# First token's scores and softmax on VectorE, the fourth batch's loads behind w2, and the first w2 piece in halves

## The chip, the cores and the metric

The kernel runs on one core of one Trainium2 chip. The metric is the device time of one execution in microseconds (us), taken as the median of three runs. An execution is also recorded by the hardware profiler; its rows are shown below. The engines are named as in the profile: PE is TensorE (matrix products; PEld its weight loads), DVE is VectorE, ACT is ScalarE, POOL is GpSimd, SP is SyncE, which issues most of the transfers (DMA).

## The reference, cut to what matters

Three layers run one after the other over 4 batches of 576 tokens. An attention through 32 memory slots per head comes first, then a mixture of 8 experts of which each token uses one, then a gated convolutional feed-forward layer.

```python
a = softmax(phi, axis=2)                     # 4 batches, 8 heads, 576 tokens, 32 slots
k_m = einsum('bhsm,bhsd->bhmd', a, k)        # head size 64
v_m = einsum('bhsm,bhsd->bhmd', a, v)
x = softmax(q @ k_m.T / 8) @ v_m             # heads side by side: 4 x 576 x 512
for b in range(4):                           # experts: 512 -> 1024 -> 512
    for s in range(576):
        fresh = argmax(x[b, s] @ w_gate)
        e = fresh if s == 0 or local_gate[b, s] < 0.5 else prev
        out[b, s] = p[e] * (relu(x[b, s] @ w1[e]) @ w2[e]); prev = e
h = relu(out @ w_in)                         # 512 -> 1024
y = (h * sigmoid(conv3(h))) @ w_out          # 3-tap convolution over the tokens, 1024 -> 512
```

The first token of a batch settles which expert is used from then on, until a token's local gate is below 0.5.

## The kernel before

**Work.** The kernel works out the first token's expert of each batch early, loads that expert's weights and runs the whole batch through it (tokens of other experts are treated at the end, by code that the change does not touch). A batch b has two units u = 2b and 2b + 1 of four heads each. For a unit, `phi` is loaded (128 x 576), its softmax is taken (`pmax`, `pexp`, `prec`), PE transposes it (`pback`, PSUM tile `pa`) and multiplies it with keys and values (`mem`, 40 matmuls of which the profile prints one or two groups, PSUM tile `pk`). ACT copies `pk` to `pm`, scaled by the softmax's sums; PE transposes that for both units (`back`, `pkt`), and the copy `vt` holds keys and values by slot. `gatew` multiplies the values with the gate's weights (`pw`, copied to `vwg`).

**First token.** `frow` multiplies the first token's queries with `vt` on PE (`pfa`); DVE scales and masks the 8 x 128 result (`fw`) and takes its maximum (`fmx`). `fexp` takes ACT's exponential and DVE's reciprocal (`fsm`, `fsl`). `fcol` turns the weights into a column with a second product (`pfb`, copied to `fcol`). `flog` multiplies it with `vwg` (`pfc`), takes the maximum (`flm`) and its index `e0i`. SP reads `e0i` to address the expert's weights.

**All tokens.** `scores` (PSUM tile `sc`), then a softmax over slots on DVE and ACT (`st`, `mx`, `sd`, `smx`, `at`), whose result is split into a high and a low part (`att`), because every large product is computed in three products of such parts. `vw` multiplies the expert's first weights with `vt` (`pv`, split into `vh` and `vl`). A hidden product (`h`) is six matmuls into `ph`; ACT's ReLU gives its high part, DVE its low part. A second product (`y`) is 24 matmuls into `py`, which ACT copies out as `ys`. The second weights come in four pieces `wb{batch}_{0..3}` of 512 KB; a load lands in a raw tile (`wb_2r` is the raw tile of piece 2), of which there are six, and `split` makes the parts: ACT the high one, DVE the low one.

**Order.** PE runs in an order written by hand. `OPENING` lists the items up to the first batch's first half, for PE, DVE, ACT and SP alike. Behind it each batch has 24 places, 8 `h`, 4 `y`, 8 `h`, 4 `y`; `order()` puts other items behind places (`FIRST` those of batch 0). In these, a scheduler orders DVE, ACT and SP by priority, except for pinned instructions, which keep the program's order. The items for the next batches are among them: with batch b's places stand the first token of batch b + 1 and the phi softmax and `mem` of batch b + 2. `needed_behind` ties the loads of a batch's phi and kv behind an earlier weight load.

**PSUM.** `pk`, `ph`, `py`, `pkt`, `pfa`, `pfb`, `pfc` share four banks; `sc`, `pa`, `pv`, `pw` share two double ones. Units 4 and 5 belong to the third batch, 6 and 7 to the fourth.

```python
def needed_behind(b):
    return None if b < 2 else "wb0_3" if b == 2 else f"wb{b - 2}_1"
```

Of the kernel before, what the change touches and what calls it, by code (L numbers as in the profile page):

```python
# [40 lines left out]
phi.0 phi.1 kv.0 kv.1 gates phi.2 phi.3 q.0.0 cload q.0.1 kv.2  # L41
pmax.0 pexp.0 pmax.1 pexp.1 prec.0 prec.1 pback.0 pback.1 mem.0 mem.1 back.0
pmax.2 pmax.3 frow.0 gatew.0 fexp.0 scores.0.0 strn.0.0 pexp.2 pexp.3 fcol.0 flog.0
smx.0.0 ssub.0.0 scores.0.1 strn.0.1 sexp.0.0 pback.2 pback.3 ssum.0.0 ahi.0.0 prec.2 prec.3 alo.0.0 mem.2
w1.0 kv.3 vw.0.0 wload.0.2 q.1.0 wload.0.3 q.1.1 nload.0 nload.1 phi.4 kv.4
h.0 vw.0.1 h.0 vw.0.2 h.0 h.0 vw.0.3 h.0 h.0 w2.0.0 h.0 h.0 smx.0.1 w2.0.1 ssub.0.1 w2.0.2 sexp.0.1
y.0 phi.5 kv.5 mem.3 ssum.0.1 w2.0.3 y.0 back.1 ahi.0.1 alo.0.1 nar.0 nload.2 y.0 gatew.1 frow.1 fexp.1 nar.1 nload.3 y.0
fcol.1
# [10 lines left out]
def order():  # L59
# [16 lines left out]
    for b in range(B):  # L76
# [39 lines left out]
def fused_kernel(tc, q, first, kv, kv_tail, phi, w1, w2, w_in, conv_w, w_out, out):  # L116
# [3 lines left out]
    with (  # L120
# [938 lines left out]
```

## Time and profile before

| | us |
|---|---|
| median of three runs | 432.62 (431.87 to 433.3) |
| the profiled execution | 434.75 |
| its span | 433.0 |
| PE busy in the span | 410.8 (95%) |
| DVE busy | 275.8 (64%) |
| ACT busy | 222.6 (51%) |

In the profile a row of the timeline reads: start, length, engine, line, operation, output <- input, partitions x elements, count, and in brackets the idle time of the engine before it and what released it. A row of the chain reads: start, length, engine and what. The granted clock is the share of full speed that PE was given in a stretch; 1.00 is 2.4 GHz and 0.50 is 1.2 GHz. The opening takes the first 38 us, the expert layer runs to 227 us, and the last layer from there to the end.

### The profile page before, as it was taken

What the parts mean: (1) busy time and instruction counts of PE and PEld (TensorE: products, weight loads), DVE (VectorE), ACT (ScalarE), POOL (GpSimd) and SP (SyncE); (2) the same over time, 40 slices, a digit from 0 to 9 for tenths busy, and PEclk for the clock granted to TensorE, in tenths of its full rate; (3) what the DMA queues carried; (4) which work ended last, traced back from release to release, by engine and by line L of the source; (5) the groups of instructions that cost most, each with busy time, mean ns of one, the idle gap of its engine ahead of it and who ended that gap; (6) DMA issues with size and microseconds to landing.
All of it is one profiled execution on the core that took longest, in us unless ns stands there. A gap on an engine that the chain in (4) does not pass through costs nothing.

```text
span 433.0 us, 8229 instructions
## 1 busy us (share of the span) xinstructions
PE 410.8 (95%) x3272; PEld 366.5 (85%) x3273; DVE 275.8 (64%) x483; ACT 222.6 (51%) x413; POOL 74.5 (17%) x123
## 2 busy tenths in 40 slices
PE   4689999969999999999999999999999999999994
PEld 2358978838998899889999988999889998999884
DVE  2378889539657898596699896178602885078600
ACT  4346565435556635654476771377423772366420
POOL 1000210131112121231010242014300133004300
PEclk9999999969999999999999999999999999999998
DMA  8979979962788359993663003200030000200012
GB/s 241 310 295 370 357 269 392 359 233 72 257 296 296 117 141 366 404 388 111 187 202 120 0 2 109 98 0 2 0 98 25 2 1 2 97 2 2 2 74 55
DMA packets 23246, 68.76 MB, mean 159 GB/s; under 512 B 3264, under 2 KB 3520, under 8 KB 23200
## 3 DMA queue, kind: packets, MB, share of 16 engines
q1 hardware_dynamic: 19616, 56.63, 37.6%
q0 software_dynamic: 3584, 11.54, 7.1%
q8 instruction: 27, 0.44, 0.4%
q14 instruction: 19, 0.16, 0.1%
HBM read 51.82 MB, written 16.33 MB: 157 GB/s over the span
## 4 chain that ended last, share of the span: by engine, by line
PE 86%; DMA 9%; ACT 1%; DVE 1%; SPq 1%; issue 1%; ACTq 0%
PE pi L159 23%; PE po L966 23%; PE py L159 21%; PE ph L159 11%; DMA kv<-in_kv 5%; DMA wb_2r<-in_w 3%; PE pk L399 2%; PE pv L421 2%; PE pl L540 1%; DMA wa_1r<-in_w 1%; PE sc L421 1%; PE pa L385 1%; SPq L340 0%; PE pfb L509 0%; DVE wb L149 0%
## 5 line engine op out<-in xcount | busy, mean ns | idle before, releaser
L159 PE MATMUL py<-h,wb 128*128 128x288 f32 x768 | 108.5, 298 | 0.7 <-DVE wb L149 0.7
L159 PEld LDWEIGHTS py<-h,wb 128*128 128x128 f32 x768 | 103.0, 188 | 5.3 <-issue 3.8
L159 PE MATMUL pi<-yh,wi 128*128 128x288 f32 x512 | 90.4, 295 | 0.0
L966 PE MATMUL po<-wo,g 128*128 128x512 f32 (+1 forms) x408 | 90.2, 377 | 0.0
L966 PEld LDWEIGHTS po<-wo,g 128*128 128x128 f32 x408 | 72.8, 188 | 13.2
L159 PEld LDWEIGHTS pi<-yh,wi 128*128 128x128 f32 x512 | 76.3, 188 | 0.9
L948 DVE SCALAR_TENSOR_TENSOR ct<-ht,convw,ct 128x575 f32<-128x575 f32 x32 | 30.9, 966 | 53.3 <-ACT ct L947 53.3
L159 PE MATMUL ph<-att,vh 128*128 128x288 f32 x256 | 54.9, 307 | 5.2 <-ACT ys L774 4.6
L159 PE MATMUL pi<-yl,wi 128*128 128x288 f32 x256 | 54.6, 295 | 0.0
L159 PEld LDWEIGHTS ph<-att,vh 128*128 128x128 f32 x256 | 41.4, 192 | 11.3 <-ACT ys L774 4.9
L931 POOL CAST tail<-g 128x128 fp32r<-128x128 f32 x32 | 22.4, 703 | 122.6 <-DVE g L149 121.9
L775 POOL DMA_DIRECT2D ydram<-ys x32 | 17.5, 547 | 150.2 <-ACT ys L774 135.8
L159 PEld LDWEIGHTS pi<-yl,wi 128*128 128x128 f32 x256 | 41.1, 188 | 0.0
L945 ACT ACTIVATE ht<-pi 128x576 f32<-128x576 f32 x32 | 20.9, 653 | 34.6 <-PE pi L159 34.5
L159 PE MATMUL ph<-att,vl 128*128 128x288 f32 x128 | 38.2, 299 | 0.2 <-DVE vl L688 0.2
L699 ACT ACTIVATE h<-ph 128x288 fp32r<-128x288 f32 x64 | 25.7, 411 | 20.3 <-PE ph L159 20.1
L700 DVE SCALAR_TENSOR_TENSOR h<-ph,h 128x288 fp32r<-128x288 f32 x64 | 28.2, 450 | 10.8 <-ACT h L699 10.5
L774 ACT ACTIVATE ys<-py 128x288 f32<-128x288 f32 x32 | 13.1, 408 | 38.4 <-PE py L159 24.8
L926 DVE TENSOR_TENSOR ct<-ht,ct 128x576 f32<-128x576 f32 x32 | 27.1, 847 | 7.8 <-ACT ct L925 7.8
L990 ACT ACTIVATE ot<-po 128x512 f32<-128x512 f32 x17 | 9.5, 598 | 43.5 <-PE po L966 43.5
L950 DVE SCALAR_TENSOR_TENSOR ct<-ht,convw,ct 128x575 f32<-128x575 f32 x32 | 28.3, 885 | 0.4
L148 ACT ACTIVATE g<-ct 128x576 fp32r<-128x576 f32 x32 | 21.7, 680 | 12.6 <-DVE ct L926 12.6
(235 smaller groups left out, 500.2 us busy)
## 6 DMA issues: line engine op xcount, KB each, us to landing
kv<-in_kv SPq DMA_DIRECT2D x16, 512.0 KB, 10.5
q<-in_q SPq DMA_DIRECT2D x8, 576.0 KB, 10.6
ydram<-ys POOLq DMA_DIRECT2D x32, 144.0 KB, 5.1
y<-ydram SPq DMA_DIRECT2D x4, 1152.0 KB, 5.8
out<-ot SPq DMA_DIRECT2D x15, 256.0 KB, 2.0
ph<-in_phi SPq DMA_DIRECT2D x8, 288.0 KB, 8.8
adram<-at POOLq DMA_DIRECT2D x8, 288.0 KB, 3.3
wa_0r<-in_w SPq DMA_DIRECT2D x4, 512.0 KB, 3.7
```

Of the source, the lines that this page charges most:

```text
L148: pin(nc.scalar.activation(hi, src, AF.Copy))
L159: pin(nc.tensor.matmul(ps, st, mv[:, cols], start=i == 0, stop=i == len(terms) - 1))
L699: nc.scalar.activation(t[:, 0, :], ps, AF.Relu)
L700: low = nc.vector.scalar_tensor_tensor(t[:, 1, :], ps, 0.0, t[:, 0, :].bitcast(F32), ALU.max, ALU.subtract)
L774: nc.scalar.activation(yt, ps, AF.Copy)
L775: stored.append(nc.gpsimd.dma_start(ydram[b, d, :, half(hf)], yt).ins)
L926: slow(f"gm.{f}").tensor_tensor(ct, ht, ct, ALU.mult)
L931: nc.gpsimd.tensor_copy(tail[:, f, :, to:to + 64], t[:, :, 512:576].bitcast(F32))
L945: nc.scalar.activation(two(ht), halves(ps), AF.Relu)
L948: nc.vector.scalar_tensor_tensor(ct[:, 1:], ht[:, :S - 1], convw[:, 0, f:f + 1], ct[:, 1:], ALU.mult, ALU.add)
L950: nc.vector.scalar_tensor_tensor(ct[:, :S - 1], ht[:, 1:], convw[:, 2, f:f + 1], ct[:, :S - 1], ALU.mult, ALU.add)
L966: nc.tensor.matmul(ps[:, cols], st[sp], w[:, mp, f % 2, cols], start=f == 0 and i == 0, stop=f == 7 and i == 2)
```

## The change

**The first token.** A new item `firstq` loads the batch's first queries, each copied to the 32 slots of its head, as a 128 x 128 tile `q0r` (four loads of 128 rows of 512 B, one for a batch). In `memory` DVE multiplies `pk`'s key half with the phi softmax's scale and with `q0r` and sums along the row, which gives a unit's 128 scores by slot straight from PSUM; ACT's copy `pm` reads the same `pk`. `prec` has one operation more, the scale divided by 8. `frow` transposes the scores on DVE and takes the maximum over 32, `fexp` takes the exponential, normalizes and transposes back to a column. The item `fcol`, the products `pfa` and `pfb`, their constants and the copies on POOL are gone.

**Order in the opening.** `frow`, `fexp` and `flog` of batch 0 now stand ahead of the last phi maximum and of the scores; `mem.2` stands behind the second hidden product instead of ahead of `vw`; the first w2 piece is split in halves behind the fourth and the fifth hidden product (`w2part`) instead of whole behind the sixth. The first hidden product takes both high terms first and those with low weights last.

**Loads.** The fourth batch's phi and kv stand behind wb1_3 instead of wb1_1. The split of piece 2 moves from place 23 to place 2 of the following batch, and is pinned.

```diff
+phi.0 phi.1 kv.0 firstq.0 kv.1 gates phi.2 phi.3 q.0.0 cload q.0.1 firstq.1 kv.2
+pmax.0 pexp.0 pmax.1 pexp.1 prec.0 prec.1 pback.0 pback.1 mem.0 mem.1 frow.0 pmax.2 fexp.0 back.0 gatew.0 flog.0
+pmax.3 pexp.2 pexp.3 scores.0.0 strn.0.0 smx.0.0 ssub.0.0 scores.0.1 strn.0.1 sexp.0.0 pback.2 pback.3
+ssum.0.0 ahi.0.0 prec.2 prec.3 alo.0.0 w1.0 kv.3 vw.0.0 wload.0.2 q.1.0 wload.0.3 q.1.1 nload.0 nload.1 phi.4 kv.4
+h.0 vw.0.1 h.0 mem.2 vw.0.2 h.0 h.0 w2part.0 vw.0.3 h.0 w2part.1 h.0 h.0 h.0 smx.0.1 w2.0.1 ssub.0.1 w2.0.2 sexp.0.1
...
-                2: [f"rtok.{b}"] * whole + each(d, "phi", "kv"),
+                2: [f"w2.{b}.2"] + [f"rtok.{b}"] * whole + of(d, "firstq") + each(d, "phi", "kv"),
...
-                8: of(c, "fcol") + [f"scores.{c}.1", f"ssoft.{c}.1"] * whole + each(d, "psoft"),
+                8: [f"scores.{c}.1", f"ssoft.{c}.1"] * whole + each(d, "psoft"),
...
-                23: [f"w2.{c}.2"] * whole + [f"q.{d}.0", f"q.{d}.1"] * (d < B),
+                23: [f"q.{d}.0", f"q.{d}.1"] * (d < B),
...
+            if low_last:
+                terms = [t for i in range(3) for t in terms[i::3]]
...
-            return None if b < 2 else "wb0_3" if b == 2 else f"wb{b - 2}_1"
+            return None if b < 2 else f"wb{b - 2}_3"
...
+            scaled[u] = ap.tile([128, 1], F32, tag="rs8", bufs=2, name=f"rs8{u}")
+            nc.vector.tensor_scalar(scaled[u], sums[u], 1.0 / np.sqrt(D).item(), None, ALU.mult)
...
+            with urgent():
+                nc.vector.scalar_tensor_tensor(q0r[b][:, g, :], pk[:, :64], scaled.pop(u), q0r[b][:, g, :],
+                                               ALU.mult, ALU.mult, accum_out=first2[:, b % 2, g:g + 1])
             nc.scalar.activation(pms[b][:, :, g, :], pk.rearrange("p (i d) -> p i d", i=2), AF.Copy, scale=rs)
...
+        def first_queries(b):
+
+            q0r[b] = ap.tile([128, 2, 64], F32, tag="q0r", bufs=2, name=f"q0r{b}")
+            with behind(needed_behind(b)):
+                nc.sync.dma_start(q0r[b].rearrange("p g d -> p (g d)"),
+                                  first_q[:, b].rearrange("h (o n) -> h o n", o=1).to_broadcast([4, 32, 128]))
...
-            nc.tensor.matmul(ps, q0s[:, b, :], kvt[b][:, 0, :], start=True, stop=True)
...
+                nc.vector.transpose(w, first2[:, b % 2, :])
                 nc.vector.tensor_reduce(nm, w, AX.X, ALU.max, negate=True)
...
-                nc.vector.tensor_scalar(sl, of_group, sm, None, ALU.mult)
-            rows0[b] = w, sl
+                nc.vector.tensor_scalar(w, w, sm, None, ALU.mult)
+                nc.vector.transpose(col, w)
...
-            nc.tensor.matmul(pc[:, 0:2], *rows0.pop(b), start=True, stop=True)
-            col = ap.tile([128, 2], F32, tag="fcol", name=f"fcol{b}")
...
-            pin = tc.keep_in_program_order if b == 0 or j == 3 else lambda ins: ins
+            pin = tc.keep_in_program_order if b == 0 or j > 1 else lambda ins: ins
...
+        def first_w2(i):
+
+            if i == 0:
+                raws0.append(fetch("wb0_0"))
+                wbs[0, 0] = wpool.tile([128, 2, 1024], F32R, tag="wb", bufs=4, name="wb0_0")
+            cols = slice(512 * i, 512 * i + 512)
+            t = wbs[0, 0]
+            split(t[:, 0, cols], t[:, 1, cols], raws0[0][:, cols])
...
+        "first_q": q.reshape(B, 2, 4, S, D)[:, :, :, 0].transpose(2, 0, 1, 3).reshape(4, B, 128),
```

The order on the engines shows the moves at three places. SP, in batch 1, behind the load of piece 1 (`wb_1r`); `q` are the third batch's queries, `ph` and `kv` the fourth batch's, `n4r` words of the last layer's weights. Before:

```order
L283 DMA wb_1r<-in_w 128x1024
L347 DMA q_0_1210<-in_q 128x1152
L333 DMA ph_1268<-in_phi 128x576
L347 DMA q_1_1212<-in_q 128x1152
L340 DMA kv_1270<-in_kv 128x1024 x2
L341 DMA kv_1270<-in_kv_tail 64x512
L333 DMA ph_1274<-in_phi 128x576
L340 DMA kv_1276<-in_kv 128x1024 x2
L341 DMA kv_1276<-in_kv_tail 64x512
L267 DMA n4r<-in_w_in 128x1024
L283 ISA
L283 DMA wb_2r<-in_w 128x1024
```

SP at the same place after (the lines are those of the changed kernel):

```order
L274 DMA wb_1r<-in_w 128x1024
L338 DMA q_0_1215<-in_q 128x1152
L338 DMA q_1_1217<-in_q 128x1152
L258 DMA n4r<-in_w_in 128x1024
L274 ISA
L274 DMA wb_2r<-in_w 128x1024
L274 ISA
L274 DMA wb_3r<-in_w 128x1024
L485 DMA q0r_1275<-in_first_q 128x1x128
L324 DMA ph_1277<-in_phi 128x576
L331 DMA kv_1279<-in_kv 128x1024 x2
L332 DMA kv_1279<-in_kv_tail 64x512
```

Both units' phi and kv moved from ahead of `n4r` and `wb_2r` to behind `wb_3r`, with the first queries ahead of them. Next, DVE in the opening, from the last phi maximum or the first row on. Before:

```order
L363 TENSOR_REDUCE nm_244<-ph_149 128x1
L489 SCALAR_TENSOR_TENSOR fw_248<-pfa_246,other 8x128
L491 TENSOR_REDUCE fmx_249<-fw_248 8x1
L499 TENSOR_SCALAR fsm_262<-fsm_262 8x1
L500 RECIPROCAL fsm_262<-fsm_262 8x1
L501 TENSOR_SCALAR fsl_263<-of_group,fsm_262 8x2
L445 STREAM_TRANSPOSE st_0_277<-sc_0_268 128x576
L512 COPY fcol_287<-pfb_285 128x2
L522 MAX flm_292<-pfc_289 1x8
L523 MAX_INDEX e0i<-flm_292,pfc_289 1x8
L524 TENSOR_SCALAR code_101<-e0i 1x1
L449 TENSOR_REDUCE mx_0_296<-st_0_277 128x18
```

DVE at the same place after:

```order
L495 STREAM_TRANSPOSE fw_239<-first_93 128x32
L496 TENSOR_REDUCE fmx_240<-fw_239 128x1
L354 TENSOR_REDUCE nm_243<-ph_141 128x1
L505 TENSOR_SCALAR fsm_245<-fsm_245 128x1
L506 RECIPROCAL fsm_245<-fsm_245 128x1
L507 TENSOR_SCALAR fw_239<-fw_239,fsm_245 128x32
L508 STREAM_TRANSPOSE fcol_246<-fw_239 128x32
L519 MAX flm_270<-pfc_267 1x8
L520 MAX_INDEX e0i<-flm_270,pfc_267 1x8
L354 TENSOR_REDUCE nm_274<-ph_143 128x1
L444 STREAM_TRANSPOSE st_0_291<-sc_0_282 128x576
L448 TENSOR_REDUCE mx_0_293<-st_0_291 128x18
```

The fourth unit's phi maximum and the first score transpose moved from ahead of `e0i` to behind it. Last, PE from the transposed phi of the fourth unit to the second hidden product. Before:

```order
L386 MATMUL pa_321<-ident,ex_282 64x128
L399 MATMUL pk_344<-kv_156,a_318 32x128 x20
L421 MATMUL pv_0_395<-wa_0r,vt_240 32x256 x8
L159 MATMUL ph_00_426<-att_337,vh_0_393 128x288 x2
L159 MATMUL ph_00_426<-att_337,vl_0_394 128x288
L159 MATMUL ph_00_426<-att_337,vh_0_393 128x288 x2
L159 MATMUL ph_00_426<-att_337,vl_0_394 128x288
L421 MATMUL pv_1_436<-wa_1r,vt_240 32x256 x8
```

PE at the same place after:

```order
L381 MATMUL pa_318<-ident,ex_279 64x128
L420 MATMUL pv_0_373<-wa_0r,vt_255 32x256 x8
L159 MATMUL ph_00_404<-att_334,vh_0_371 128x288 x4
L159 MATMUL ph_00_404<-att_334,vl_0_372 128x288 x2
L420 MATMUL pv_1_414<-wa_1r,vt_255 32x256 x8
L159 MATMUL ph_01_425<-att_334,vh_0_371 128x288 x2
L159 MATMUL ph_01_425<-att_334,vl_0_372 128x288
L159 MATMUL ph_01_425<-att_334,vh_0_371 128x288 x2
L159 MATMUL ph_01_425<-att_334,vl_0_372 128x288
L394 MATMUL pk_435<-kv_152,a_315 32x128 x20
```

The third unit's `pk` moved from ahead of `pv` to behind the second hidden product, and the first hidden product's two `vl` terms moved to its end.

## Rows read from the trace of the kernel before

**Rows 1.** The page's chain that ended last: share of the span by engine:

```profile
PE 86%; DMA 9%; ACT 1%; DVE 1%; SPq 1%; issue 1%; ACTq 0%
```

**Rows 2.** Waits of PE from 60 to 130 us: engine, line, releaser, total, times, longest:

```profile
PE ph L159 <- ACT ys L774: 4.6, 1, 4.6
```

**Rows 3.** Timeline around the gap of PE in batch 1:

```profile
85.78 0.39 PE L485 MATMUL pfa<-vt,q0s 128*8 128x128 f32 x2
89.34 1.06 ACT L148 ACTIVATE wb<-wb_2r 128x1024 fp32r<-128x1024 f32 x1 [7.33 <-DMA wb_2r<-in_w]
...
90.75 0.85 PE L159 MATMUL ph<-att,vh 128*128 128x288 f32 x2 [4.58 <-ACT ys L774]
```

**Rows 4.** Chain that ended last, in order of time: start, length, engine, what:

```profile
42.39 1.36 PE pk L399 x40
...
54.46 0.31 PE pfb L509 x2
54.77 1.00 PE ph L159 x6
...
57.58 1.09 PE pl L540 x8
...
77.07 12.25 DMA wb_2r<-in_w
...
90.75 1.81 PE ph L159 x6
92.56 2.06 PE pl L540 x8
94.62 1.49 PE ph L159 x6
```

**Rows 5.** Windows: length, busy time (instructions) by engine, granted clock, DMA share, GB/s:

```profile
86.20:88.00 1.80, 0.00 (x0) 0.00 (x0) 0.00 (x0) 0.00 (x0) 0.00 (x0) 1.00 1.02 414
88.00:90.00 2.00, 0.00 (x0) 0.00 (x0) 0.00 (x0) 0.66 (x1) 0.00 (x0) 0.72 0.52 213
90.00:95.00 5.00, 4.25 (x16) 2.47 (x17) 2.79 (x6) 2.04 (x6) 3.73 (x7) 0.50 0.54 191
```

**Rows 6.** Timeline of SP in batch 1:

```profile
75.56 0.33 SPq L267 DMA_DIRECT2D n4r<-in_w_in  x1
```

**Rows 7.** Transfers from 59 to 90 us: issues, KB each, median us to landing:

```profile
ph<-in_phi SPq DMA_DIRECT2D x2, 288.0 KB, 10.9
```

**Rows 8.** Timeline of DVE in batch 1, split of the first w2 piece:

```profile
73.43 1.23 DVE L149 TENSOR_TENSOR wb<-wb_0r,wb 128x1024 fp32r<-128x1024 f32 x1
```

**Rows 9.** Timeline of the opening:

```profile
17.44 0.58 PE L485 MATMUL pfa<-vt,q0s 128*8 128x128 f32 x2 [0.56 <-ACT vt L414]
...
18.06 0.28 DVE L489 SCALAR_TENSOR_TENSOR fw<-pfa,other 8x128 f32<-8x128 f32 x1 [1.34 <-PE pfa L485]
...
18.44 0.19 ACT L432 ACTIVATE vwg<-pw 128x18 f32<-128x18 f32 x1 [1.14 <-PE pw L421]
...
19.70 0.76 DVE L445 STREAM_TRANSPOSE st<-sc 128x576 f32<-128x576 f32 x1
...
20.73 0.25 PE L519 MATMUL pfc<-vwg,fcol 128*1 128x8 f32 x4 [0.25 <-DVE fcol L512]
...
21.30 0.15 DVE L523 FIND_INDEX8 e0i<-flm,pfc 1x8 uint32<-1x8 f32 x1
...
25.14 2.31 PE L399 MATMUL pk<-kv,a 128*32 128x128 f32 x36
...
27.44 0.76 DVE L643 TENSOR_TENSOR att<-at,att 128x576 fp32r<-128x576 f32 x1 [0.27 <-ACT att L640]
...
29.85 0.30 PE L159 MATMUL ph<-att,vl 128*128 128x288 f32 x1
...
39.18 1.06 PE L159 MATMUL py<-h,wb 128*128 128x288 f32 x6 [0.73 <-DVE wb L149]
```

**Rows 10.** Windows, one microsecond of the opening:

```profile
25.00:26.00 1.00, 1.00 (x19) 0.80 (x20) 0.93 (x3) 0.69 (x2) 0.00 (x0) 1.00 1.05 430
```

More of the change, by code (lines that the diff above doesn't have):

```diff
@@ L40 @@
 OPENING = """
[L41 to L48, printed above, removed]
+phi.0 phi.1 kv.0 firstq.0 kv.1 gates phi.2 phi.3 q.0.0 cload q.0.1 firstq.1 kv.2
[3 more added lines that the diff above has]
+h.0 vw.0.1 h.0 mem.2 vw.0.2 h.0 h.0 w2part.0 vw.0.3 h.0 w2part.1 h.0 h.0 h.0 smx.0.1 w2.0.1 ssub.0.1 w2.0.2 sexp.0.1
+y.0 firstq.2 phi.5 kv.5 mem.3 ssum.0.1 w2.0.3 y.0 back.1 ahi.0.1 alo.0.1 nar.0 nload.2 y.0 gatew.1 frow.1 fexp.1 nar.1 nload.3 y.0
 """.split()
@@ L113, with fused_kernel @@
 ON_POOL = {"gs.3", "gs.4", "gs.6"}
-def fused_kernel(tc, q, first, kv, kv_tail, phi, w1, w2, w_in, conv_w, w_out, out):
+def fused_kernel(tc, q, first, first_q, kv, kv_tail, phi, w1, w2, w_in, conv_w, w_out, out):
     nc = tc.nc
@@ L149, in split, with matmul3 @@
             pin((eng or nc.vector).tensor_tensor(lo, src, hi.bitcast(F32), ALU.subtract))
-        def matmul3(outs, pairs, pin=lambda ins: ins):
+        def matmul3(outs, pairs, pin=lambda ins: ins, low_last=False):
             terms = []
@@ L494, in first_weights @@
         def first_weights(b):
-            w, nm = rows0[b]
-            sm, sl = (ap.tile([8, n], F32, tag=t, name=f"{t}{b}") for t, n in (("fsm", 1), ("fsl", 2)))
+            w, nm = rows0.pop(b)
+            sm = ap.tile([128, 1], F32, tag="fsm", name=f"fsm{b}")
+            col = cols0[b] = ap.tile([128, 32], F32, tag="fcol", name=f"fcol{b}")
             with urgent():
@@ L695, in hidden @@
             matmul3([(ps, half(hf))],
-                    [((hi[:, f % 4, g, :], lo[:, f % 4, g, :]), (at[:, g, 0, :], at[:, g, 1, :])) for g in range(2)])
+                    [((hi[:, f % 4, g, :], lo[:, f % 4, g, :]), (at[:, g, 0, :], at[:, g, 1, :])) for g in range(2)],
+                    low_last=f"{name}{hf}{f}" == "000")
             t = fps[-1].tile([128, 2, HALF], F32R, tag="h", bufs=8, name=f"h{name}_{hf}{f}")
@@ L711, in load_gates @@
         def load_gates():
-            nc.sync.dma_start(firsts, first)
-            for g in range(2):
-                nc.gpsimd.tensor_copy(q0s[rows(g), :, 4 * g:4 * g + 4],
-                                      firsts[rows(g), 36:].rearrange("p (b h) -> p b h", h=4))
+            nc.sync.dma_start(wgl.rearrange("p h n -> p (h n)"), first)
         cw_raw = work("cw_raw", I32)[:, :48]
@@ L840, in fused_kernel @@
             "w2": lambda b, j: stage_w2(lambda: src_w2(expert(b)), j, f"wb{b}_{j}", b),
+            "w2part": lambda i: i or loads["w2"](0, 0),
             "win": lambda kc: stage_w1(lambda: src_in, kc, f"wi{kc}"),
@@ L1009, in fused_kernel @@
         late[0].__exit__(None, None, None)
-_INS = ["q", "first", "kv", "kv_tail", "phi", "w1", "w2", "w_in", "conv_w", "w_out"]
+_INS = ["q", "first", "first_q", "kv", "kv_tail", "phi", "w1", "w2", "w_in", "conv_w", "w_out"]
 def kernel(q, k, v, phi, moe_w_gate, moe_w_local, moe_w1, moe_w2, moe2_w_in, moe2_conv_w, moe2_w_out):
```

38 lines of the change are left out of this document (11 added, 27 removed), and 2 rows, old and new, of the table FIRST.

## The prediction

> **What bounds the kernel now.** I read the chain of work that ended last first. TensorE (PE) carries 86% of it and transfers 9% [rows 1], so a change is worth what it takes off PE's own row of work or out of PE's waits. In the table of PE's waits, the stretch from 60 to 130 us has one entry, 4.6 us long [rows 2]; after 100 us there is none. So I read the timeline there. PE ends its last matmul, a `pfa`, at 86.17 us and starts the next at 90.75; that one is released by the copy `ys` on ScalarE (ACT), which frees a PSUM bank. The copy had not waited for PE: it stood behind the split of `wb_2r` in ACT's row, and the split had waited 7.33 us for its load [rows 3]. The load is a piece of the chain itself: issued at 77.07, landed 12.25 us later [rows 4].
>
> The stall costs more than its length. The granted clock reads 0.72 from 88 to 90 us and 0.50 (1.2 instead of 2.4 GHz) from 90 to 95 [rows 5], and the first matmuls after the gap take 1.81, 2.06 and 1.49 us, where the same groups a half batch earlier took 1.00, 1.09 and again 1.0 (the third by the first's row, the same six matmuls) [rows 4].
>
> The other place is the opening, where PE is not yet the bound: it waits for softmaxes on VectorE (DVE), for the expert index `e0i` and for the loads that hang on it [rows 9].
>
> **The stall, and why it should go.** In before SP issues the fourth batch's phi and kv loads ahead of `n4r` and `wb_2r`: two units of 288 + 1152 KB, 2.88 MB. At the 414 GB/s of 86 to 88 us [rows 5] that is about 7.0 us of queue ahead of `wb_2r`. The change ties these loads to wb1_3 instead, so `n4r`, `wb_2r` and `wb_3r` stand ahead of them. What then holds `wb_2r` is a free raw buffer, which comes when DVE's split of the first piece ends, 73.43 + 1.23 = 74.66 us [rows 8], and SP's own row; `n4r`, which stands just ahead of it, went at 75.56 in before, itself behind the moved loads [rows 6]. I take the issue at 74.7. With 7.0 us less queue ahead it lands 12.25 - 7.0 = 5.25 us later, at 80; with before's full 12.25 us it would be 87. Its split also moves, from place 23 to place 2 of the next batch, behind the third hidden product. PE has done two of these at 85.78, where `pfa` (place 1) stands [rows 3], and a third takes 1.0, so ACT asks at about 86.8, less the 1 us or so that is saved ahead of it. Even the late bound costs ACT 1 us, which four PSUM banks cover. So the whole wait goes: **4.58 us**.
>
> With no gap the clock should stay up: 0.81 + 0.97 + 0.49 = **2.3 us** [rows 4]. Had the clock fallen for another reason than the pause it would stay lost; it reads 1.00 up to 88 us, two into the pause [rows 5], so I take the whole.
>
> What is late next? The fourth batch's phi now goes at about 77.5, behind `wb_3r`, and at 10.9 us to landing [rows 7] is there at 88.4, its second unit by 90. DVE's maxima over it stand at place 8. Ahead of it PE has six more hidden products behind 85.78 at 1.0 and the route product at 1.1 [rows 4], which is 93 us without a stall, and a second product of 24 matmuls besides, no more than 4 us by the 1.0 for six, so up to 97. I cost the move at nothing; the cover is 3 to 7 us.
>
> **The first token on DVE.** Each of batches 1 to 3 loses `pfa` and `pfb` from PE. All six lie in PE's row: `pfb` at 0.31 us three times (one row stands for them [rows 4]), `pfa` at 0.39 in the row of 85.78 [rows 3] and twice at the same 0.32 as `pfb` within 0.01: 0.93 + 1.03 = **1.95 us**.
>
> What DVE gains: per unit one multiply with accumulation out of PSUM and one scaling of a column, per batch two small transposes; it loses two small operations and a copy. The new multiply has 64 columns; the nearest row, one from PSUM of 8x128, took 0.28 us [rows 9]. These run beside PE, but ACT's copy `pm` of the same bank now stands behind the multiply, so 0.3 us is added from `pk` to `pm` in every unit, and a DVE that is busy hands its delay to ACT. Moreover the `wb_2` split (1.06 us on ACT [rows 3], 1.23 on DVE [rows 8]) now lies among hidden products, which want both engines. Nothing in the trace of before shows this coupling. Least is 0 (the banks cover all); most is one split's length passed to PE, 1.2, and 0.3 more. I take **-0.4**, nearer to nothing, because PE showed no wait for a hidden product's `h` in 60 to 130 us [rows 2].
>
> **The opening.** In before `pfc` starts at 20.73, behind `fcol`, and `e0i` ends at 21.45. Its other input, `vwg`, was ready at 18.63 already, and was itself behind `pfa` (0.58) [rows 9]. After: no `pfa`, 0.28 for the multiply ahead of `pm`, so `vwg` at about 18.3, and 0.72 from there as before: `e0i` at 19.05, **2.4 us** earlier. DVE's own chain (multiply, transpose, maximum, a 0.76 us phi maximum, sum, reciprocal, multiply, transpose) ends at 18.2 if the transposes take 0.2, so it is just covered. But the gain isn't kept. DVE now does one phi maximum and the first score transpose (both 128x576, 0.76 each by the transpose's row) behind `e0i` instead of ahead, with a few gaps 1.6. So the first attention is 0.75 us earlier, not 2.4: DVE's low parts end at 27.5 instead of 28.20 [rows 9]. From there the first hidden product is quicker. In before `mem.2` (the pk group of 25.14 to 27.45) stood ahead of `pv` and the first product ended at 30.15; now weights land 2.4 us earlier, `pv` is done, the high terms run first, and the low terms wait only for DVE's first part of `vl` (128x256, about half of a 128x576 operation, 0.4) and take 0.4: end at about 28.3. That is 1.85 earlier. Set against it, mem.2's 40 matmuls now lie among the products: 1.36 us [rows 4], and 1.43 the other time that 40 stand together. The wait of the second product for the split `wb`, 0.73 [rows 9], should go, since the piece is split in halves, two products earlier and one. And the first-query load stands ahead of the second unit's kv: 128 rows of 512 B, 64 KB, which at 430 GB/s [rows 10] is 0.15 us, taken as 0.2.
>
> Then PE's pace. The granted clock reads 1.00 at 25 us [rows 10], yet matmuls are slow there: 36 of pk took 2.31 us at 25.14, 40 took 1.36 at 42.39 [rows 4, 9]. That pk group and `pv` keep PE at work right up to the first product, and by 29.85 a matmul is back at 0.30 [rows 9]. In the changed order PE has little between the last phi transposes and the first product but `pv`. So the first hidden products may run at the slow pace: 0.8 for one product (1.81 against 1.00) and 0.6 for a `pv` group, 1.4 together. I take half, 0.7, and keep 0 and 1.7 (`mem.2` slow as well) as ends. Opening: 1.85 - 0.2 - 1.43 + 0.73 - 0.7 = **+0.25**, between -1.7 and +1.5.
>
> The load's cost is 0.2 only if the row spreads over the DMA engines as others do. The Trainium skill speaks against it: DMA: Bandwidth & Descriptors, "Rules for kernel authors", says that a small outermost dimension confines the whole transfer to at most so many engines. No row of before has a load of this form. The source here has 4 outermost, so by that rule a quarter of the engines carry all; this is rival E.
>
> **Sum.** 4.58 + 2.3 + 1.95 - 0.4 + 0.25 = 8.7 us. The profiled execution took 434.75 (span 433.0), which would become 426.1. That run is 2.1 above the median of 432.62 of the three timed runs; I take the same 8.7 from the median: **423.9 us**.
>
> **Rivals.**
> A, the forecast: stall and clock loss gone, opening near zero. 423.9. For it: one transfer's queue position explains the whole stall.
> B, the opening turns bad: slow pace to its full 1.7 instead of 0.7, and 0.6 of the 0.73 wait stays because DVE is behind with `vl`, the multiply and two half splits. 423.9 + 1.6 = 425.5. For it: the pause ahead of the products; against: the two half splits are no more work than the one that made the 0.73 wait, and stand earlier.
> B', the opening pays: quick pace from the start and a shorter softmax chain, 1.25 better. 422.7.
> C, the change doesn't do what it says: `wb_2r` is still late, because the raw buffer or SP's row holds it, or another load takes its place. Then 4.58 + 2.3 come back. 430.8. Against: the order moved is plain, and the buffer was free at 74.7.
> D, slower: the fourth batch's phi, now last, comes late. DVE's maxima at place 8 wait, the split of wb1_3 may stand behind them, and PE stops where the fourth second product needs it, at about 93 + 3 x 4 = 105 us, with the clock falling again. The 8.7 gained is spent when phi lands past 105 + 8.7 - 2.3 = 111.4, over 30 us after its issue; landing at 114 gives 435.2. `wb_2r` took 12.25 in the fullest queue [rows 4].
> E, the first-query load on 4 of 16 engines: four times 0.15, 0.6 instead of 0.2, all of it ahead of pk in the opening. 424.3.
>
> **Chances.** A 0.50, B 0.18, B' 0.12, E 0.10, C 0.07, D 0.03. The range 420.5 to 427.5 takes in A, B, B' and E; its low end is the opening at +1.5 with no coupling (423.9 - 1.25 - 0.4 = 422.3), and a stall in the timed runs up to 1.8 costlier than in the profiled one; its high end B with the coupling at its most, 1.5 instead of 0.4 (426.6), and 0.9 of the clock loss kept. C and D, 0.10, are left out. A difference of about 0.3%, 1.3 us, can be told from none. Faster by more than that: A, B, B', E and nearly all of C, 0.93; within, 0.04; slower, 0.03.
>
> **What would show it.** Right: `wb_2r` issued near 75 and landed before 84; no PE wait over 1 us between 75 and 110; granted clock 1.00 there; the first `pi` of the second FFN 8 to 9 us earlier. In the opening `e0i` ends near 19.2, and the first second product starts its long run within 0.8 us of 39. It is wrong if PE waits for `ys`, `h` or `wb` between 80 and 110 us, if the hidden products up to 38 us run near 1.8 us each for more than two of them, or if ACT's `pm` waits a microsecond and more for DVE in batches 1 to 3 and PE for ACT behind it.

## The result

The changed kernel took 426.99 us (median of four runs, 426.71 to 427.5); the kernel before, beside it, 432.73. The ratio is 0.987, with a 95% interval of 0.9851 to 0.989. So the direction was right and the time lies in the stated range, 3.1 us above the 423.9 that was forecast. The profiled execution of the changed kernel took 426.71 us with a span of 425.0, where before had 434.75 and 433.0: between the two profiled executions the gain is 8.0 us, near the 8.7 of the sum. Between the medians it is 5.7. This gap is the first thing to explain.

The chain of the changed kernel: the share of transfers, 9% in [rows 1], is down to 2%.

```profile
PE 92%; DMA 2%; DVE 2%; ACT 1%; SPq 1%; issue 0%; ACTq 0%
```

In batch 1 the gap is gone. SP issues `wb_2r` at 74.22 us, the fourth batch's phi follows at 76.78; ACT comes to the split at 86.52 without a wait for the load, where [rows 3] had 7.33 us, and the clock stays up, where [rows 5] read 0.72 and 0.50. SP's timeline, then ACT's, then windows (length, busy time by engine, granted clock, DMA share, GB/s):

```profile
74.22 0.34 SPq L274 DMA_DIRECT2D wb_2r<-in_w  x1
...
76.78 0.45 SPq L324 DMA_DIRECT2D ph<-in_phi  x1
```

```profile
86.21 0.41 ACT L697 ACTIVATE h<-ph 128x288 fp32r<-128x288 f32 x1 [0.38 <-PE ph L159]
86.52 1.05 ACT L146 ACTIVATE wb<-wb_2r 128x1024 fp32r<-128x1024 f32 x1
```

```profile
86.00:88.00 2.00, 2.00 (x16) 1.18 (x14) 1.18 (x3) 1.76 (x3) 2.00 (x5) 1.00 1.04 421
88.00:90.00 2.00, 2.00 (x27) 1.37 (x26) 1.89 (x3) 0.48 (x3) 0.33 (x1) 1.00 1.04 414
```

PE's table of waits from 60 to 130 us, one row of 4.6 us in [rows 2], is empty. From the first matmul of batch 1's hidden products (84.11 in before, 83.64 after) to the first of its second products (99.95, now 92.10) PE needs 7.4 us less, where the stall, the slow stretch and one `pfa` were 7.3.

The opening gave next to nothing. The index `e0i` is there 2 us earlier, as its row against [rows 9] shows (21.30), but the first long run of second products starts at 39.36, where before had it at 39.18, and `mem.3`, the 40 `pk` matmuls behind that run, starts at 42.53, where before had it at 42.39 [rows 4]. The index's row in the timeline:

```profile
19.25 0.15 DVE L520 FIND_INDEX8 e0i<-flm,pfc 1x8 uint32<-1x8 f32 x1
```

and the chain of the changed kernel (start, length, engine, what):

```profile
27.21 1.87 PE ph L159 x6
29.08 1.03 PE pv L420 x16
30.12 1.72 PE ph L159 x6
31.83 1.25 PE pk L394 x36
...
39.36 3.17 PE py L159 x24
42.53 1.36 PE pk L394 x40
...
218.96 16.00 PE pi L159 x120
```

The first two hidden products took 1.87 and 1.72 us and the `pv` between them 1.03; the same groups are 1.00 [rows 4] and 0.59 at the quick pace. From `mem.3` on the gain is there: the first `pi`, with which the last layer opens, starts 8.3 us earlier. In the chain of before it stands at:

```profile
227.24 16.00 PE pi L159 x120
```

So the stretch from `mem.3` to the first `pi`, in which the stall and the first tokens of batches 1 to 3 lie, took 184.85 us in before and 176.43 after, 8.42 less. The experiments are compared by this stretch too, because it leaves out the opening.

### The profile page after: what moved, and what is told of

Read it like the earlier page. It is cut to its first block, busy times and chain, and to the rows that moved or that the text cites. A ratio compares the mean times of both kernels' runs of the same rounds, so it can differ in the third digit from the quotient of the medians.

```text
span 425.0 us, 8216 instructions
## 1 busy us (share of the span) xinstructions
PE 406.2 (96%) x3256; PEld 364.2 (86%) x3257; DVE 276.8 (65%) x505; ACT 221.9 (52%) x414; POOL 74.8 (18%) x121
## 4 chain that ended last, share of the span: by engine, by line
PE 92%; DMA 2%; DVE 2%; ACT 1%; SPq 1%; issue 0%; ACTq 0%
PE py L159 25%; PE pi L159 24%; PE po L973 23%; PE ph L159 12%; PE pk L394 2%; DMA kv<-in_kv 2%; PE pv L420 2%; PE pl L537 1%; PE sc L420 1%; SPq L331 0%; PE pa L380 0%; PE pkt L411 0%; DVE wb L147 0%; PE pt L549 0%; PE pw L420 0%
## 5 line engine op out<-in xcount | busy, mean ns | idle before, releaser
L957 DVE SCALAR_TENSOR_TENSOR ct<-ht,convw,ct 128x575 f32<-128x575 f32 x32 | 28.4, 886 | 0.4
```

The costliest lines, as they stand in the source:

```text
L957: nc.vector.scalar_tensor_tensor(ct[:, :S - 1], ht[:, 1:], convw[:, 2, f:f + 1], ct[:, :S - 1], ALU.mult, ALU.add)
```

## The experiments

Each starts from the kernel before or from the changed kernel, with the edit shown. Times are medians of the timed runs. Experiments 1 to 4 ran on one chip beside runs of before, and so did 5 to 8 and 9 to 12.

**1. The kernel before, once more.** No edit.

> The kernel before, unchanged, profiled once more and timed. Theory S (the wait for wb_2r differs from execution to execution, and the profiled execution at 434.75 us had a long one): the new profiled execution is nearer to the median of 432.7, by 1 to 2.5 us, and its one long PE wait near 86 us and the slow stretch behind it are shorter by as much: a wait of 2 to 3.6 us instead of 4.58. Rival U (the wait is the same each time, and the 2.1 us between that profiled execution and the median lie elsewhere): a wait of 4.4 to 4.8 us again, whatever the time. Timed: 432.7 within 0.6.

433.21 us in the profiled execution, 434.04 in the median of 12, where 432.7 within 0.6 was expected; 23 runs of before beside it had a median of 433.46 and lay between 430.72 and 436.03. The long wait is 3.6 us this time, not 4.6 (waits of PE, then the timeline):

```profile
PE ph L159 <- ACT ys L774: 3.6, 1, 3.6
```

```profile
88.44 1.06 ACT L148 ACTIVATE wb<-wb_2r 128x1024 fp32r<-128x1024 f32 x1 [6.38 <-DMA wb_2r<-in_w]
...
89.84 0.85 PE L159 MATMUL ph<-att,vh 128*128 128x288 f32 x2 [3.64 <-ACT ys L774]
```

So theory S: the stall differs from one execution to the next. With 0.94 us less wait, and the low clock over a shorter stretch, this execution was 1.54 us shorter than the one that the forecast was made on. All of the difference lies between `mem.3` (42.42 here, 42.39 there) and the first `pi` (225.55, 227.24). All 61 timed runs of before spread over 5.6 us with a median of 433.5, so the profiled 434.75 was a costly one and the three runs at 432.62 were cheap ones. What was not borne out is the size: I had expected to meet runs at the median with a wait of 2 to 3.6 us, and 3.6 is the top of that.

**2. Only the loads' part.** The kernel before with `needed_behind` and the split's place changed.

```diff
-    21: "gatew.2 vw.1.0 vw.1.1 w2.1.0", 22: "vw.1.2 vw.1.3 w2.1.1", 23: "w2.1.2 q.2.0 q.2.1 save.0",
+    21: "gatew.2 vw.1.0 vw.1.1 w2.1.0", 22: "vw.1.2 vw.1.3 w2.1.1", 23: "q.2.0 q.2.1 save.0",
...
-            return None if b < 2 else "wb0_3" if b == 2 else f"wb{b - 2}_1"
+            return None if b < 2 else f"wb{b - 2}_3"
...
-                2: [f"rtok.{b}"] * whole + each(d, "phi", "kv"),
+                2: [f"w2.{b}.2"] + [f"rtok.{b}"] * whole + each(d, "phi", "kv"),
...
-                23: [f"w2.{c}.2"] * whole + [f"q.{d}.0", f"q.{d}.1"] * (d < B),
+                23: [f"q.{d}.0", f"q.{d}.1"] * (d < B),
...
-            pin = tc.keep_in_program_order if b == 0 or j == 3 else lambda ins: ins
+            pin = tc.keep_in_program_order if b == 0 or j > 1 else lambda ins: ins
```

> The kernel before with only the loads' part: the fourth batch's phi and kv behind wb1_3, the split of piece 2 at place 2 and pinned. First token and opening as before. Both theories: no PE wait over 1 us between 75 and 110 us, and a profiled span near 433.0 - 4.6 - 2.3 = 426.1. Theory S: in the timed runs it takes off only 6.9 - 2.1 = 4.8 us, so 427.9 (427.3 to 428.5). Rival U: it takes off 6.9, so 425.8, and the rest of the change costs 1.2 us.

427.0 us (five runs, 426.95 to 428.16) against 433.46, a ratio of 0.9852 (0.9821 to 0.9883); span 426.4, against the 426.1 expected. No wait over 1 us is left between 75 and 110. The timed gain of 6.5 lies between the two theories' 4.8 and 6.9 and nearer to the rival's; the median of before beside it was 0.8 above the one that the expectation started from. Neither number was met: 427.0 is 0.3 below the range of S and 1.2 above U. `wb_2r` was issued at 74.53 and landed 6.0 us later (the sum had 74.7 and 5.25):

```profile
74.53 0.34 SPq L283 DMA_DIRECT2D wb_2r<-in_w  x1
```

```profile
wb_2r<-in_w SPq DMA_DIRECT2D x1, 512.0 KB, 6.0
```

**3. Everything but the loads' part.** The changed kernel with that edit taken back.

> The changed kernel with only the loads' part undone: phi and kv of the fourth batch behind wb1_1 again and the split of piece 2 at place 23, unpinned. The stall comes back under both. Theory S: timed 427.0 + 4.8 = 431.8 (431 to 432.8), that is 0.9 faster than before, by the products pfa and pfb taken off PE (1.95) less coupling (0.4) and a slower opening (0.3). Rival U: 427.0 + 6.9 = 433.9, slower than before.

434.41 us, 433.03 to 436.24 in 12 runs, against 433.46 of before: a ratio of 1.0014 (0.9991 to 1.0036). Without the loads' part the rest of the change shows no gain in these runs. The profiled execution, at 436.24, has a stall of 7.8 us, since here `wb_2r` went at 79.57 instead of 77.07 and landed 12.7 us later:

```profile
PE ph L159 <- ACT gated_rows L539: 7.8, 1, 7.8
```

```profile
79.57 0.35 SPq L274 DMA_DIRECT2D wb_2r<-in_w  x1
```

```profile
92.27 1.06 ACT L146 ACTIVATE wb<-wb_2r 128x1024 fp32r<-128x1024 f32 x1 [8.34 <-DMA wb_2r<-in_w]
```

In before a wait of 3.6 us went with 433.21 and one of 4.6 with 434.75; here, in another kernel, one of 7.8 goes with 436.24. Theory S's number (431.8) was 2.6 too low and the rival's (433.9) 0.5; both took the stall for that of before, and in this execution it was 3.2 us longer, which is more than the first token gains (6). Why `wb_2r` went later here stays open.

**4. mem.2 ahead of the first hidden product.** The changed kernel with one item moved.

```diff
-h.0 vw.0.1 h.0 mem.2 vw.0.2 h.0 h.0 w2part.0 vw.0.3 h.0 w2part.1 h.0 h.0 h.0 smx.0.1 w2.0.1 ssub.0.1 w2.0.2 sexp.0.1
+mem.2 h.0 vw.0.1 h.0 vw.0.2 h.0 h.0 w2part.0 vw.0.3 h.0 w2part.1 h.0 h.0 h.0 smx.0.1 w2.0.1 ssub.0.1 w2.0.2 sexp.0.1
```

> The changed kernel with mem.2 (40 matmuls) moved ahead of the first hidden product, behind the first pv: work for PE in the gap from 26.2 to 27.2 us. Theory P (the opening lost its gain to PE's slow pace: the first two hidden products took 1.87 and 1.72 us, pv 1.03): the first product starts 0.5 to 1 us later but at the quick pace, the 1.34 us of mem.2 leave the stretch behind, and the first second product starts 1.5 to 2.3 us earlier than 39.2; timed 425.0 (424.6 to 425.6). Rival Q (what comes after is bound by DVE and ACT, by the loads of w1, or PE stays slow anyway): within 0.4 us of 427.0, or slower.

425.86 us (424.53 to 426.91 in five runs). The first long run of second products started at 38.88 here, only 0.5 us earlier than in the changed kernel: the second unit's kv came 0.6 us later than there, and the quick pace set in at 30.7. Inconclusive by itself, so it ran again beside the changed kernel (7).

**5. The changed kernel, once more.** No edit.

> The changed kernel, unchanged, beside the next kernel on one chip. Theory S: 427.0 within 0.6 and runs no further apart than 1.5 us, since no transfer's arrival sets a wait.

426.54 us, 425.89 to 428.11 in five runs, span 424.5, against 433.58 of before (11 runs, 432.65 to 434.83): a ratio of 0.9843 (0.9821 to 0.9864). With the first four runs the changed kernel has 426.7 in nine runs within 2.2 us, wider than expected. The reason given for the narrow spread was wrong as well: a transfer still sets the opening. The second unit's `pk` waits for its kv and starts at 14.32 in the first profile and at 13.75 in this one; over all fourteen profiles it starts between 12.93 and 16.02.

**6. Only the loads' part, once more.** The kernel of 2.

> The kernel before with only the loads' part, once more, to be compared on one chip with the changed kernel: the difference is what the first token on VectorE and the new opening are worth. Theory V (worth what the two profiled spans say, 426.4 - 425.0): 1.0 to 1.8 us slower than the changed kernel. Rival W (worth nothing: the 1.95 us of pfa and pfb are given back): within 0.4 us of it.

427.92 us in the median, 1.4 above the changed kernel, where V said 1.0 to 1.8. But its six runs lie between 425.73 and 430.95, and the five of 2 had 427.0, so this is unclear as a difference of times. The chains are clearer. Of `mem.3` and the first `pi`, in 2 and then in 6:

```profile
42.23 1.36 PE pk L399 x40
...
220.59 16.00 PE pi L159 x120
```

```profile
45.17 1.36 PE pk L399 x40
...
223.45 16.00 PE pi L159 x120
```

From one to the other is 178.36 and 178.28 us; in the two profiles of the changed kernel it is 176.43 and 176.33 (42.34 to 218.67 in 5), and in the six other profiles with the first token on VectorE and no stall it lies between 176.1 and 176.8. So behind the opening the first token on VectorE is worth 1.9 to 2.0 us, and rival W falls; what blurs it in the times lies ahead of `mem.3`. The profiled execution at 430.95 shows where that spread comes from; its span is 2.8 us longer than in 2, and all of it is there by 42 us. The first hidden product of 2, then of 6, in their timelines:

```profile
28.50 0.53 PE L159 MATMUL ph<-att,vh 128*128 128x288 f32 x2 [0.58 <-ACT vh L686]
```

```profile
28.80 0.85 PE L159 MATMUL ph<-att,vh 128*128 128x288 f32 x2 [0.57 <-ACT vh L686]
...
29.94 0.68 PE L159 MATMUL ph<-att,vh 128*128 128x288 f32 x2
...
31.82 0.85 PE L159 MATMUL ph<-att,vh 128*128 128x288 f32 x2
```

The same two matmuls took 0.53 us in one execution and 0.85 in the other. The opening's pace is thus a second thing that differs from execution to execution, in kernels without the stall too. A long pause of PE does not explain it: in 6 PE was at work throughout from 24 to 28 us and then idle for the 0.57 us of its row, in 2 for 0.58. Windows of 6 (the number behind the length is PE's busy time):

```profile
24.00:26.00 2.00, 2.00 (x29) 1.54 (x31) 1.86 (x5) 0.89 (x3) 0.00 (x0) 1.00 1.00 375
26.00:28.00 2.00, 2.00 (x40) 0.93 (x32) 1.57 (x6) 1.05 (x2) 0.00 (x0) 1.00 0.93 307
```

**7. mem.2 early, once more.** The kernel of 4, beside 5.

> The changed kernel with mem.2 ahead of the first hidden product, once more, beside the changed kernel. Theory P (PE's slow pace in the opening): 0.6 to 1.4 us faster than the changed kernel. Rival Q: within 0.4.

424.8 us (423.7 to 426.7 in five runs) against 426.54, so 1.7 less, where P said 0.6 to 1.4. In the profiled execution, the fastest of the five, the first hidden product's four high matmuls took 0.79 us instead of 1.39, and the first second product started at 36.29. Chain, then timeline:

```profile
36.29 3.20 PE py L159 x24
```

```profile
27.33 0.79 PE L159 MATMUL ph<-att,vh 128*128 128x288 f32 x4
```

**8. PE kept at work in two waits.** The kernel of 4 with eight matmuls that nobody reads.

```diff
-pmax.3 pexp.2 pexp.3 scores.0.0 strn.0.0 smx.0.0 ssub.0.0 scores.0.1 strn.0.1 sexp.0.0 pback.2 pback.3
+pmax.3 pexp.2 pexp.3 scores.0.0 strn.0.0 smx.0.0 ssub.0.0 scores.0.1 strn.0.1 sexp.0.0 pback.2 warm.0 pback.3 warm.1
...
+        def warm(i):
+            ps = bank(f"warm{i}")
+            for _ in range(4):
+                nc.tensor.matmul(ps[:, :128], ident, ident, start=True, stop=True)
...
```

> The kernel with mem.2 ahead of the first hidden product, and besides two groups of four 128x128 matmuls whose results nobody reads, ahead of the fourth unit's phi transposes and ahead of the first pv, where PE waits: added work of about 2.2 us that is to lie in waits. Theory P (PE is at the lower level because it was idle shortly before, and the opening's stretch of products is bound by that): the quick pace comes before the first hidden product, so that this product takes 1.0 to 1.2 us instead of 1.7 to 1.9 and mem.2 1.4 instead of 2.5; the first second product starts 1.5 to 2.5 us earlier than without the added matmuls, and the time falls by as much. Rival Q (softmax and loads bind the opening): the matmuls only delay, 0 to 1 us slower.

423.77 us (423.0 to 424.75 in five runs): 2.8 less than the changed kernel, with work added, and 1.0 less than 7, whose runs overlap with these. The quick pace is there before the first product. Windows of the changed kernel's second profile (5) and of this one:

```profile
26.00:28.00 2.00, 1.37 (x5) 1.33 (x6) 1.72 (x7) 0.86 (x3) 0.00 (x0) 0.50 0.96 373
28.00:30.00 2.00, 2.00 (x21) 0.92 (x20) 0.46 (x1) 0.76 (x2) 0.00 (x0) 0.50 1.03 422
...
32.00:34.00 2.00, 2.00 (x52) 1.39 (x45) 0.51 (x3) 0.60 (x2) 0.00 (x0) 1.00 1.07 282
```

```profile
20.00:22.00 2.00, 1.92 (x28) 0.85 (x20) 1.97 (x3) 0.87 (x2) 0.00 (x0) 0.50 0.48 122
22.00:24.00 2.00, 2.00 (x14) 1.86 (x13) 1.91 (x4) 1.01 (x2) 0.00 (x0) 0.75 0.98 340
24.00:26.00 2.00, 1.49 (x21) 1.33 (x25) 1.86 (x5) 1.06 (x4) 0.00 (x0) 1.00 0.90 266
```

In 5 the granted clock is at 0.50 (1.2 GHz) from 26 to 32 us, after PE had worked 0.74 us of the two from 22 and 0.67 of the two from 24. In 8 PE has no pause from 22 to 25.4 us and next to none before, and the clock is at 1.00 (2.4 GHz) from 24 on. `mem.2` then takes 1.43 us, where it took 1.97 in 7 and 2.31 in before [rows 9], and the first product's high matmuls 0.81:

```profile
26.53 1.43 PE L394 MATMUL pk<-kv,a 128*32 128x128 f32 x40
...
27.89 0.81 PE L159 MATMUL ph<-att,vh 128*128 128x288 f32 x4
```

Rival Q falls: the opening's stretch of products was bound by PE's pace, and with PE kept at work ahead of them the quick one was there in time. The first second product starts at 36.93, which is 1.95 us earlier than in 4, as P said, but later than the 36.29 of 7, where the second unit's `pk` started 1.2 us earlier (13.53, here 14.72). From the second unit's `pk` to `mem.3`, which leaves that landing out, it is 28.2 and 28.6 us in the changed kernel, 27.2 and 26.0 in 4 and 7, and 25.4 both here and in 12. That PE's pause is the whole cause isn't shown: 4 and 7 are one kernel and got the quick pace at 30.7 and 26.6 us, and 6 had the slow one behind four microseconds of unbroken work, where 2, the same kernel, had the quick one.

**9. The split's place undone.** The changed kernel with the split of piece 2 back at place 23, unpinned.

```diff
-    21: "gatew.2 vw.1.0 vw.1.1 w2.1.0", 22: "vw.1.2 vw.1.3 w2.1.1", 23: "q.2.0 q.2.1 save.0",
+    21: "gatew.2 vw.1.0 vw.1.1 w2.1.0", 22: "vw.1.2 vw.1.3 w2.1.1", 23: "w2.1.2 q.2.0 q.2.1 save.0",
...
-                2: [f"w2.{b}.2"] + [f"rtok.{b}"] * whole + of(d, "firstq") + each(d, "phi", "kv"),
+                2: [f"rtok.{b}"] * whole + of(d, "firstq") + each(d, "phi", "kv"),
...
-                23: [f"q.{d}.0", f"q.{d}.1"] * (d < B),
+                23: [f"w2.{c}.2"] * whole + [f"q.{d}.0", f"q.{d}.1"] * (d < B),
...
-            pin = tc.keep_in_program_order if b == 0 or j > 1 else lambda ins: ins
+            pin = tc.keep_in_program_order if b == 0 or j == 3 else lambda ins: ins
```

> The changed kernel with the split of w2's piece 2 back at place 23 and unpinned; phi and kv of the fourth batch stay behind wb1_3. Theory L (the place in SP's row alone makes the stall): wb_2r is issued near 74 and there by about 81 to 83, so ACT meets it with a wait of 1.5 us at most and PE with none over 0.5; timed within 0.6 us of 426.8. Rival M (the split's place matters too, because ACT in its order stands at the split and holds the copies back): a PE wait of 1 to 3 us between 80 and 90, and 428 to 430.

426.23 us (425.9 to 428.0 in four runs), like the changed kernel, and no PE wait there. ACT meets the load at 81.36 without a wait, 5.5 us after its issue at 75.83:

```profile
81.36 1.06 ACT L146 ACTIVATE wb<-wb_2r 128x1024 fp32r<-128x1024 f32 x1
```

So with the loads moved, the split's later place adds nothing. The stretch from `mem.3` to the first `pi` is even the shortest here, 176.10 us, and PE has no wait from 45 to 232 us. The profiled execution, at 428.0, is the longest of the four; in it the second unit's kv came late, and its `pk` starts at 16.02.

**10. The loads' place undone.** The changed kernel with the old `needed_behind`; the split stays at place 2.

```diff
-            return None if b < 2 else f"wb{b - 2}_3"
+            return None if b < 2 else "wb0_3" if b == 2 else f"wb{b - 2}_1"
```

> The changed kernel with phi and kv of the fourth batch behind wb1_1 again; the split of piece 2 stays pinned at place 2. Theory L: wb_2r is issued at 77 to 80 and lands near 89 to 92, so the stall is back: ACT meets it at place 2 (86 us), PE waits 2 to 6 us as its banks fill, and the granted clock falls to 0.50 behind it; timed 431 to 434.5. Rival M: the later place covers it, under 429.

428.54 us in four runs between 425.91 and 431.65. Here theory L's number was wrong, and the rival's right for the median, though not for all four runs: the load is late as L says (issued at 78.40), ACT does wait 4.08 us for it, yet PE loses only 1.6, and the clock reads 1.00 throughout 84 to 94 us.

```profile
85.30 0.41 ACT L697 ACTIVATE h<-ph 128x288 fp32r<-128x288 f32 x1 [0.38 <-PE ph L159]
89.80 1.06 ACT L146 ACTIVATE wb<-wb_2r 128x1024 fp32r<-128x1024 f32 x1 [4.08 <-DMA wb_2r<-in_w]
```

```profile
PE ph L159 <- ACT gated_rows L539: 1.6, 1, 1.6
```

At place 2 the copies that free the banks are already done when ACT stops, so PE has banks to go on with. In 3, with the split at place 23, ACT stood at it from 83.9 us on with the copies of `ph` still behind it; here three of those were done by 85.7. Against 3, with the same order of loads, that is 5.9 us less. Either half of the loads' part takes most of the stall away. With the order alone (9) no wait is left; with the place alone one of 1.6 us is, and runs that lie 5.7 us apart.

**11. The first-query load from 128 rows.** The changed kernel, with each head's row standing 32 times in memory.

```diff
-                                  first_q[:, b].rearrange("h (o n) -> h o n", o=1).to_broadcast([4, 32, 128]))
+                                  first_q[b])
...
-        "first_q": q.reshape(B, 2, 4, S, D)[:, :, :, 0].transpose(2, 0, 1, 3).reshape(4, B, 128),
+        "first_q": q.reshape(B, 2, 4, S, D)[:, :, :, 0].transpose(0, 2, 1, 3).reshape(B, 4, 128).repeat(32, axis=1),
```

> The changed kernel with the first-query load's source laid out as 128 rows (each head's row 32 times in memory) instead of 4 rows repeated by the access pattern. Theory E (the load of 4 rows lies on 4 of 16 DMA engines and delays the second unit's kv): pk of the second unit starts 0.2 to 0.5 us earlier than the 13.75 to 14.3 of the changed kernel's profiles, time 0.2 to 0.5 less. Rival (the load's cost is its bytes): no difference beyond 0.4 either way.

425.38 us (424.88 to 426.26 in four runs), 1.2 to 1.6 less than the two medians of the changed kernel; that is more than theory E expected, and the changed kernel did not run beside it. The kernel of 9, which differs from the changed one only in the split's place, did run beside it and took 426.23, 0.85 more, in runs that overlap with these. `pk` of the second unit starts at 12.93 in its profile, earlier than in any other; but in 12, with the same layout, it starts at 13.58, and with the 4 rows it started anywhere from 13.29 (in 3) to 16.02. So what the layout is worth in time is not shown. The packets tell the two layouts apart. Of the pages, the packets of the changed kernel, then of this one:

```profile
DMA packets 23775, 69.02 MB, mean 162 GB/s; under 512 B 3280, under 2 KB 4048, under 8 KB 23728
```

```profile
DMA packets 23823, 69.02 MB, mean 163 GB/s; under 512 B 3328, under 2 KB 4096, under 8 KB 23776
```

The bytes are the same, and there are 48 small packets more: 12 for each of the four loads. The Trainium skill, DMA: Bandwidth & Descriptors, "Why a DMA increments its semaphore by 16 and not by 1", says that of a transfer issued this way each engine that takes part posts an increment of its own; 4 for a load against 16 would be just these 12. By that rule, the trace agrees that the load as it was changed lay on 4 engines.

**12. Both together.** The kernel of 8 with the load of 11.

> The kernel with mem.2 ahead of the first hidden product and the two groups of unread matmuls, and the first-query load laid out as 128 rows as well: the two combined. Theory P: again the quick pace before the first hidden product, 423.8 within 0.7 and 2.5 to 3.5 below the changed kernel. Theory E would add 0.2 to 0.5 to that. Rival Q: the former run's gain was a chance of the opening, and this one is within 1 us of the changed kernel.

422.93 us (422.48 to 423.8 in six runs), a ratio to before of 0.9755 (0.9715 to 0.9796), span 421.2. This is the best version: 3.6 us below the changed kernel's 426.54, which did not run beside it, and 10.6 below before, with runs that lie within 1.3 us. It is a little below theory P's range and fits it with the 0.2 to 0.5 that theory E would add. How much of the last 0.8 against 8 is the load's is not settled.

## Why the prediction came out as it did

**The stall** was right step by step. The issue at 74.7 was at 74.22; ACT's call for the load at 86.8 came at 86.52; the landing after 5.25 us could not be seen where nobody waited for it, and was 6.0 in experiment 2 and 4.9 in 6. The wait of 4.58 and the slow stretch of 2.3 are gone. By the stretch from `mem.3` to the first `pi` they were worth 184.85 - 178.3 = 6.5 us, with 0.3 for the split's new place already taken off, in the execution that the forecast was made on, and 183.13 - 178.3 = 4.8 in that of experiment 1. Nothing took their place: the fourth batch's phi, which was to land 10.9 us after 77.5, landed 6.6 us after 76.78. Rivals C and D did not come. That the load's order alone is enough (9), and that the place alone is most of it (10), I had not separated; the text costed them as one.

**The first token.** `pfa` and `pfb` are gone from the chain, and 2 and 6 against the changed kernel give 1.9 to 2.0 us for it (6), which is the whole 1.95. Of the coupling, ACT's `pm` did wait for DVE, 2.0 us in one case where in before it had waited 0.98 for `pk`, and PE did not feel it. What PE felt is one wait of 0.34 us in batch 3, behind the split of `wb_2r` now standing among hidden products:

```profile
184.84 0.54 PE L159 MATMUL ph<-att,vh 128*128 128x288 f32 x2 [0.34 <-DVE h L698]
```

The table of waits has it in 2 and 6 too, where the first token is the old one, and not in 9, where the split is at its old place. So it belongs to the split. The -0.4 was about the right size, but all of it that shows came from the split and none from the new multiply.

**The opening** is where the working was wrong, and the net of it came out near by luck: +0.25 was forecast, and `mem.3` starts 0.14 us later and 0.05 earlier in the two profiles (42.53 and 42.34 against 42.39). The index came 2.05 us earlier instead of 2.4, or 2.33 counted from the second unit's `pk`, which started 0.28 later than in before; and the wait of 0.73 for the split `wb` did go. But the slow pace took more than the full price of rival B: 1.87 - 1.00 in the first product, 0.44 in `pv` and 0.73 in the second product, 2.0 us, where I had taken 0.7. By difference, the other terms were about 1 us better than costed; which of them is not shown. I had set half of that price for want of a row; the rows for the price were there, and PE's pause ahead of the first product was named. Experiments 7, 8 and 12 show that what PE does ahead of the products decides much of the pace that they get, with the limit said in 8.

The working also took the head of the opening as fixed, and it is not: the second unit's `pk` starts at 12.9 to 16.0 us. From there to `mem.3` the old opening took 28.4 to 28.8 us in three profiles, with 31.4 in the slow one of 6, and the changed opening 28.1 to 28.9 in six, so by itself it is worth a few tenths of a microsecond at most. Of rival E the packets in 11 bear out the 4 engines; its price can't be told from that scatter.

**The sum and the median.** The sum fits the execution that it was made on: 434.75 - 8.7 = 426.1, and the profiled execution of the changed kernel took 426.71. Without the opening it was 8.43, and the stretch from `mem.3` to the first `pi` became 8.42 shorter; so close a fit of one pair of executions is partly chance, since the stall's length is. The step that failed is the next one, "I take the same 8.7 from the median". The stall is a wait for a transfer, and differs between executions: 3.6 and 4.6 us in two profiled executions of before. The longer of the two, 1.2 us above the median of all runs, was the one that the sum was made on; the prediction had allowed for timed runs with a costlier stall than that, and it was the other way round. Of the 3.1 us between forecast and result, 1.2 is the profiled execution standing above before's median of 433.5 in 61 runs, 0.9 the first three runs standing below it, 0.7 the sum itself (0.4 the opening, 0.3 the last layer, whose length from the first `pi` on varies by 0.4 among the profiles), and 0.3 the changed kernel's median standing above its own profiled run. Against the larger count the gain is about 6.8 us: 433.5 to 426.7. That the time lies in the range is in part luck: its high end was made for rival B with the coupling at its most, and what filled it is this step.

What stays open: why the quick pace comes at different times in executions of one kernel, what the first-query load costs, and how the stall was spread over the 61 runs of before, of which two have a profile. The medians alone would have left the first token open too: 427.4 in the eleven runs of 2 and 6, 426.7 in nine of the changed kernel, 0.7 apart and less than the spread of either.

## What to carry to other kernels

A stall that hangs on a transfer's arrival varies from run to run: take its price from several executions, and don't subtract one profile's sum from another set's median. Where runs scatter, cut the profiles at two instructions that all the kernels have in common, and compare the stretch between them. Order loads by when they are needed, and put the step that waits for a load behind the copies that free the other engine's buffers, so that a late load costs little. Before a stretch of matrix products, look at whether TensorE had a pause; here a few matmuls that nobody reads, in waits that were there anyway, were cheaper than the slow pace behind.

## What was not expected of the hardware

The granted clock's column can be silent on the opening. In the first profile of the changed kernel it reads 1.00 from 27 to 28 us, where the second one reads 0.50 from 26 on (8), and in both the first product's four high matmuls take 1.39 us. In 6 it reads 1.00 through the slow product too. So in the openings of these profiles the durations are the evidence for the pace, and the column alone is not. The window of the first profile, then the matmuls in the first and in the second:

```profile
27.00:28.00 1.00, 0.79 (x3) 0.75 (x4) 1.00 (x4) 0.43 (x2) 0.00 (x0) 1.00 1.02 410
```

```profile
27.21 1.39 PE L159 MATMUL ph<-att,vh 128*128 128x288 f32 x4 [1.04 <-ACT vh L683]
```

```profile
26.63 1.39 PE L159 MATMUL ph<-att,vh 128*128 128x288 f32 x4 [1.39 <-ACT vh L683]
```
